# Gated linear attention, GLU and expert layer on one core: scans over four head pairs in one instruction, three more tiles turned by TensorE, low weight parts on VectorE, another opening order

## The chip, the cores and the metric

One core of a Trainium2 chip runs the whole program. The metric is device time in microseconds (us) from launch to end. The program has five engines that work in parallel and wait for each other by semaphores: PE (TensorE, matrix products), DVE (VectorE), ACT (ScalarE), POOL (GpSimd) and SP (SyncE), which issues the transfers between the main memory and the on-chip memory. Each engine takes its instructions strictly in the order in which the program holds them.

## The reference

Three layers follow one another on 4 sequences of 768 tokens with 8 heads of 48 features (3072 tokens of 384 features in all):

```
state = alpha[t] * state + outer(k[t], v[t])      # per head, 48 x 48
y[t]  = q[t] @ state
x  = rms_norm(y) * g
z  = (silu(x @ w_gate) * (x @ w_val)) @ w_out     # 384 -> 1536 -> 384
e  = argmax(z @ r_gate);  out = p_e * sigmoid((z @ r_ogate)[e]) * (relu(z @ w1[e]) @ w2[e])   # 8 experts
```

## The kernel before, in words

**Tiles.** The 3072 tokens are 24 tiles of 128. Three tiles form a group of 384 columns, so there are eight groups. Attention is computed in chunks: for a tile, the running products of alpha along its 128 tokens (backward `Z`, forward `A`) turn the recurrence into matrix products. q is multiplied by the forward product, k by the backward one; then come the scores (L392), the masked scores (L402), the output (L423, L427), the state (L448) and the normalised output turned round (L469), which feeds the GLU.

**Turning.** alpha, q and k must stand with features on partitions and the 128 tokens along the free dimension, four pairs of heads side by side (4 x 128 columns). Tiles 0 to 4 (`NAT` = 5) are loaded as rows, turned by PE with four products against the identity for each of a, k, q (L248, into the PSUM tile `ps_n`), and read from there. Tiles 5 to 23 are loaded in twelve blocks (`load_tile`) and turned by DVE (L344).

**Scans.** `after_scan` (L273) and `upto_scan` (L287) are scans of DVE, one for each pair of heads: four of 127 and four of 128 elements for a tile, with a product and a reciprocal of 4 elements between them (L281, L282).

**Weights.** The GLU's weights come as 36 chunks of 64-bit words. For each, DVE puts a float together (L491, L494, L497), ACT rounds it to the high part (L516, L543), and the low part is float minus high part. For chunks 4 to 17 (`LP` = (4, 18)) the low part is made by PE (L503 adds the float, L504 subtracts the high part, both into `ps_l`) and copied by ACT (L505); for the other 22 chunks DVE subtracts (L507). Each GLU product is three products: high by high, low by high, high by low (L571, L605).

**Order.** The first three tiles are written out by hand in `START` (a, r, k, q: turn and scan; s, n, y, d, x: score, key turn, output, state, turn of x; c: a step of conversions; w: idle products `junk` on PE). After that a loop over the GLU's products interleaves attention stages (`due`), steps of preparing later tiles (`PRN` for a slot) and steps of converting weights (`CR` for a slot). `SEATS` gives PSUM banks in the opening. A scheduler then orders each engine's instructions; the kinds in `K0` to `K2` keep the order in which they were written.

From about 640 us on the expert layer runs (L996, L997, L1012); the change doesn't touch it.

Of the kernel before, what the change touches and what calls it, by code (L numbers as in the profile page):

```python
# [8 lines left out]
F32 = mybir.dt.float32  # L9
# [3 lines left out]
AF = mybir.ActivationFunctionType  # L13
ALU = mybir.AluOpType
# [37 lines left out]
def gla_glu_moe_kernel(  # L52
# [29 lines left out]
    GT = 3  # L82
# [20 lines left out]
    ident = const.tile([P, P], F32, name="ident")  # L103
# [73 lines left out]
    for nm, pad in (("a", 1.0), ("q", 0.0), ("k", 0.0)):
        t_ = att.tile([P, NP, TW * D], F32, name=f"blk_{nm}")
        for r in (32, 96):
            nc.vector.memset(t_[r:r + 32, :, TW * D - 32:TW * D - 16], pad)  # L180
        blk[nm] = t_
# [18 lines left out]
    junk = [psM.tile([P, P], F32, tag='o2', name='junk')]  # L200
# [64 lines left out]
    SIDE = {(2, "A"): ("wgle", 0), (2, "qT"): ("wgle", 1), (2, "kT"): ("wgle", 2),  # L265
            (1, "aT"): ("wvhe", 0), (1, "P0"): ("wvhe", 1), (1, "P1"): ("wvhe", 2),
            (1, "kn"): ("wghe", 0), (1, "xn"): ("wghe", 1), (2, "v"): ("wghe", 2)}

    def after_scan(Z, al, p):

        pace('sc' + str(now[0]), nc.vector.tensor_tensor_scan(out=Z[:, p, P - 2::-1], data0=al[:, p, P - 1:0:-1],  # L273
                                                data1=ones_f.to_broadcast([P, P - 1]),
                                                initial=1.0, op0=ALU.mult, op1=ALU.mult))

    def ends(t, Z, al):

        en = att.tile([P, NP, 1], F32, tag="en", name="en", bufs=4)
        rc = att.tile([P, NP, 1], F32, tag="rc", name="rc", bufs=2)  # L280
        pace('sc' + str(now[0]), nc.vector.tensor_tensor(out=en, in0=al[:, :, 0:1], in1=Z[:, :, 0:1], op=ALU.mult))  # L281
        pace('sc' + str(now[0]), nc.vector.reciprocal(out=rc, in_=en))  # L282
        return en, rc

    def upto_scan(A, al, rc, p):

        pace('sc' + str(now[0]), nc.vector.tensor_tensor_scan(out=A[:, p, :], data0=al[:, p, :], data1=ones_f.to_broadcast([P, P]),  # L287
                                                initial=rc[:, p, :], op0=ALU.mult, op1=ALU.mult))

    QM, SM, LP = (CFG[x] for x in ("QM", "SM", "LP"))  # L290

    def prework_nat(t):
        Z = seat_of(t, "aT", [P, NP, P], CFG["ZBUF"])
        A = seat_of(t, "A", [P, NP, P], CFG["ABUF"])
        qT = seat_of(t, "qT", [P, NP, P], 2)
        kT = seat_of(t, "kT", [P, NP, P], 2)
        nc.gpsimd.memset(Z[:, :, P - 1:P], 1.0)
        ps = {}

        def turn_a():  # L300
            now[0] = t
            ps[0] = turn_nat(t, 0)
            for p in range(NP):
                after_scan(Z, ps[0], p)
            en, ps["rc"] = ends(t, Z, ps[0])
            pre[t] = (en, qT, kT)
# [25 lines left out]
    def prework(t):  # L332
        if t < NAT:
            w = prework_nat(t)
            for x in CFG['NO']:
                yield w[x]
            return
        aT = att.tile([P, NP, P], F32, tag="aT", name="aT", bufs=CFG["ZBUF"])
        Z = att.tile([P, NP, P], F32, tag="A", name="Z", bufs=CFG["ABUF"])
        qT = att.tile([P, NP, P], F32, tag="qT", name="qT", bufs=2)  # L340
        kT = att.tile([P, NP, P], F32, tag="kT", name="kT", bufs=2)

        def tr(dst, nm):
# [12 lines left out]
        for p in range(0, NP, 2):
            def sc(p=p):
                for pp in (p, p + 1):
                    after_scan(Z, aT, pp)
            yield sc  # L360

        def en():
            e_, ps["rc"] = ends(t, Z, aT)
            pre[t] = (e_, qT, kT)
        ps = {}
        yield en
        for p in range(0, NP, 2):
            def up(p=p):
                for pp in (p, p + 1):
                    upto_scan(aT, aT, ps["rc"], pp)  # L370
            yield up
# [948 lines left out]
```

## Time and profile before

| | us |
|---|---|
| median of 3 runs (lowest, highest) | 890.61 (889.08, 892.56) |
| the profiled execution's own time | 891.49 |
| its span, first to last instruction | 889.8 |
| PE busy in the span | 866.0 |
| DVE busy | 502.3 |
| ACT busy | 329.0 |
| POOL busy | 139.9 |

The span leaves out 1.69 us of the profiled execution's time around the first and last instruction. An instruction's duration overlaps with the next one's: what an instruction takes from its engine is read from one start to the next. [...]

### The profile page before, as it was taken

How to read it: one execution, taken by the hardware profiler on the slowest of the kernel's cores; microseconds unless marked ns; L12 is line 12 of the kernel's file. 1: busy time of each engine (PE TensorE's matmuls, PEld its weight loads, DVE VectorE, ACT ScalarE, POOL GpSimd, SP SyncE). 2: the span in 40 equal slices, each digit the busy share in tenths (PEclk: the TensorE clock that was granted, in tenths of full speed). 3: DMA queues.
4: the chain of work that ended last, by engine and by line, in shares of the span. 5: the costliest groups of instructions: out<-in, count | busy, mean ns of one | idle time of the engine just before them, and what ended most of it. 6: DMA issues, size and time to landing. Idle time of an engine off the chain costs nothing.

```text
span 889.8 us, 15748 instructions
## 1 busy us (share of the span) xinstructions
PE 866.0 (97%) x6048; PEld 826.0 (93%) x6048; DVE 502.3 (56%) x1181; ACT 329.0 (37%) x714; POOL 139.9 (16%) x175
## 2 busy tenths in 40 slices
PE   7999999999999999999999999999999999999994
PEld 6788899999999999999999999999998999999994
DVE  7679798558775655665675673244444443444330
ACT  1545554233333422332333343324234442445331
POOL 2000000000110010010010001013023343344331
PEclk7789999999999999999999999999999999999998
DMA  9825661637232222232222100005045264256510
GB/s 192 210 75 156 175 197 39 165 96 199 74 97 58 52 77 58 60 85 54 55 69 58 43 12 25 2 23 165 1 169 185 78 209 135 70 190 196 167 50 24
DMA packets 117485, 89.95 MB, mean 101 GB/s; under 512 B 49435, under 2 KB 112540, under 8 KB 117408
## 3 DMA queue, kind: packets, MB, share of 16 engines
q1 hardware_dynamic: 112944, 79.44, 33.5%
q0 software_dynamic: 4464, 9.48, 3.0%
q8 instruction: 48, 0.79, 0.4%
q14 instruction: 29, 0.24, 0.1%
HBM read 73.09 MB, written 16.07 MB: 100 GB/s over the span
## 4 chain that ended last, share of the span: by engine, by line
PE 86%; issue 4%; DMA 3%; DVE 2%; POOL 1%; ACT 1%; SPq 1%; POOLq 0%; ACTq 0%; DVEq 0%
PE ps_o L605 18%; PE ps_g L571 18%; PE ps_v L571 17%; PE ps_b L1012 8%; PE ps_h L571 7%; PE ps_s L392 4%; PE ps_y L427 3%; DMA st<-in_moe_w_dram 3%; PE ps_y L423 2%; PE ps_st L448 1%; PE ps_k L412 1%; PE ps_l L503 1%; PE ps_x L469 1%; SPq L880 1%; PE ps_n L248 1%
## 5 line engine op out<-in xcount | busy, mean ns | idle before, releaser
L582 DVE TENSOR_TENSOR tt<-tt,ps_v 128x384 f32<-128x384 f32 x96 | 52.8, 550 | 129.5 <-PE ps_v L571 122.6
L585 ACT ACTIVATE hh<-tt 128x384 fp32r<-128x384 f32 x96 | 50.2, 523 | 127.8 <-DVE tt L582 127.4
L563 ACT ACTIVATE tt<-ps_g 128x384 f32<-128x384 f32 x96 | 47.2, 492 | 127.5 <-PE ps_g L571 119.6
L571 PE MATMUL ps_g<-xh,wgh 128*128 128x384 f32 x192 | 68.5, 357 | 1.5 <-ACT xh L476 1.5
L1012 PE MATMUL ps_b<-w2a,h 128*128 128x384 f32 (+2 forms) x336 | 67.4, 339 | 1.3 <-ACT h L996 1.0
L997 DVE SCALAR_TENSOR_TENSOR h<-ps_h,h 128x256 fp32r<-128x256 f32 (+6 forms) x72 | 38.1, 531 | 52.7 <-ACT h L996 49.6
L571 PE MATMUL ps_v<-xh,wvh 128*128 128x384 f32 x192 | 67.3, 351 | 0.2 <-ACT wvh L516 0.2
L605 PE MATMUL ps_o<-wol,hh 128*128 128x400 f32 x192 | 66.7, 348 | 0.0
L605 PE MATMUL ps_o<-woh,hh 128*128 128x400 f32 x192 | 66.5, 355 | 0.0
L591 DVE TENSOR_TENSOR hl<-tt,hh 128x384 fp32r<-128x384 f32 x96 | 54.5, 567 | 21.0 <-ACT hh L585 20.4
L571 PE MATMUL ps_g<-xl,wgh 128*128 128x384 f32 x192 | 65.8, 343 | 0.0
L571 PE MATMUL ps_g<-xh,wgl 128*128 128x384 f32 x192 | 65.7, 342 | 0.0
L1012 PE MATMUL ps_b<-w2b,h 128*114 128x384 f32 (+3 forms) x336 | 65.2, 338 | 0.3 <-ACT h L996 0.2
L571 PE MATMUL ps_v<-xh,wvl 128*128 128x384 f32 x192 | 65.2, 340 | 0.0
L434 POOL TENSOR_SCALAR ss<-ss 128x1 f32<-128x1 f32 x24 | 5.0, 208 | 382.7 <-ACT xn L433 374.7
L571 PE MATMUL ps_v<-xl,wvh 128*128 128x384 f32 x192 | 64.8, 337 | 0.0
L605 PE MATMUL ps_o<-woh,hl 128*128 128x400 f32 x192 | 64.0, 344 | 0.0
L1012 PEld LDWEIGHTS ps_b<-w2a,h 128*128 128x128 f32 (+2 forms) x336 | 57.5, 181 | 2.5 <-ACT h L996 1.5
L1012 PEld LDWEIGHTS ps_b<-w2b,h 128*114 128x114 f32 (+3 forms) x336 | 57.4, 175 | 2.5 <-ACT h L996 1.0
L571 PE MATMUL ps_h<-x,w1b 128*128 128x456 f32 (+3 forms) x288 | 58.4, 343 | 0.6 <-DVE h L997 0.6
L996 ACT ACTIVATE h<-ps_h 128x256 fp32r<-128x256 f32 (+6 forms) x72 | 33.4, 468 | 63.5 <-PE ps_h L571 57.5
L571 PE MATMUL ps_h<-x,w1a 128*128 128x256 f32 (+3 forms) x288 | 53.4, 327 | 0.0
(279 smaller groups left out, 2029.7 us busy)
## 6 DMA issues: line engine op xcount, KB each, us to landing
st<-in_moe_w_dram SPq DMA_DIRECT2D x64, 384.0 KB
bucket<-zero SPq DMA_DIRECT2D x8, 772.0 KB
stg<-in_moe_w_gate_dram SPq DMA_DIRECT2D x12, 384.0 KB
stg<-in_moe_w_val_dram SPq DMA_DIRECT2D x12, 384.0 KB
stg<-in_moe_w_out_dram SPq DMA_DIRECT2D x12, 384.0 KB
v<-in_v_dram SPq DMA_DIRECT2D x23, 192.0 KB
blk_a<-in_alpha_dram SPq DMA_DIRECT2D x38, 96.0 KB
blk_q<-in_q_dram SPq DMA_DIRECT2D x38, 96.0 KB
```

The source lines that it names most:

```text
L392: nc.tensor.matmul(ps[hh][:, p, :], lhsT=kT[r, p, :], rhs=qT[r, p, :], start=True, stop=True)
L423: nc.tensor.matmul(ps[:, p * 2 * D:p * 2 * D + 2 * D], lhsT=qT[:, p, :], rhs=S_[:, p, :], start=(p == 0), stop=False, skip_group_check=True)
L427: nc.tensor.matmul(ps[u, h * D:h * D + D], lhsT=Pt[h % 2][:, h // 2, u], rhs=vt[t][:, h, :], start=first, stop=True, skip_group_check=True)
L563: nc.scalar.activation(tt, ps, AF.Silu)
L571: nc.tensor.matmul(ps, lhsT=a_[:, kc, :], rhs=b_[:, kc, :], start=(n == 0), stop=(n == 3 * KD - 1))
L582: nc.vector.tensor_tensor(out=tt, in0=tt, in1=ps, op=ALU.mult)
L585: nc.scalar.activation(hh, tt, AF.Copy)
L591: nc.vector.tensor_tensor(out=hl, in0=tt, in1=f(hh), op=ALU.subtract)
L605: nc.tensor.matmul(obank[s][i], lhsT=a_[:, sl], rhs=weight(b_, j), start=(j == j0 and n == 0), stop=(j == j1 - 1 and n == 2))
L996: nc.scalar.activation(hh[:, 0, :], ps, AF.Relu)
L997: nc.vector.scalar_tensor_tensor(out=hh[:, 1, :], in0=ps, scalar=0.0, in1=f(hh[:, 0, :]), op0=ALU.max, op1=ALU.subtract)
L1012: ins = nc.tensor.matmul(ob2[u][i][0:r], lhsT=hh[:, a_, sl], rhs=we[p][b_][:, j, :], start=(j == 0 and m == 0), stop=(j == KF2 - 1 and m = ...
```

## The change

The scans of the four head pairs become one: position 0 of each pair gets factor 0 in alpha's tile, and a second operand `begin`, zero elsewhere, sets the start value there (1 going backward, 1/Z going forward). Two small writes and a copy are added for it, and the forward scan of tiles 0 to 4 is written straight into q's tile, so that their tile `A` is gone. Tiles 5, 6 and 7 (`PET` = 8) are loaded as rows and turned by PE, copied out by ACT. `LP` is empty: all 36 low parts are made by DVE. The idle products have 512 columns instead of 128. `START`, `LOADS`, `SEATS`, `CR`, `PRN`, `TS`, `AHEAD` and the kept kinds are other numbers; one buffer instead of two for the backward products.

```diff
-    'START': 'a0 c r0 w6 a1 q0 k0 k1 r1 q1 w0 s0 s0 a2 c y0 s1 r2 k2 q2 y0 w0 s1 x0 y1 w4 y1 x1 ...',
+    'START': 'a0 r0 c a1 w6 q0 k0 k1 r1 q1 w0 s0 s0 a2 y0 s1 r2 c q2 y0 w0 s1 x0 k2 y1 w4 y1 x1 ...',
-    'LP': (4, 18),
+    'LP': (0, 0),
-    'AHEAD': 1,
+    'AHEAD': 0,
-    'CR': [3, 3, 3, 2],
-    'PRN': [1, 2, 1, 1],
+    'CR': [3, 4, 3, 4],
+    'PRN': [1, 2, 1, 2],
-    'ABUF': 2,
+    'ABUF': 1,
-    'TS': 2,
+    'TS': 3,
+    'PET': 8,
...
+    begin = att.tile([P, NP, P], F32, name="begin")
+    nc.gpsimd.memset(begin, 0.0)
...
-    def after_scan(Z, al, p):
-        ... nc.vector.tensor_tensor_scan(out=Z[:, p, P - 2::-1], data0=al[:, p, P - 1:0:-1],
-                                         data1=ones_f.to_broadcast([P, P - 1]), initial=1.0, op0=mult, op1=mult)
+    def after_scan(Z, al):
+        pace(k_, nc.vector.tensor_copy(en, al[:, :, 0:1]))
+        pace(k_, nc.vector.memset(al[:, :, 0:1], 0.0))
+        pace(k_, nc.vector.memset(begin[:, 1:, 0:1], 1.0))
+        pace(k_, nc.vector.tensor_tensor_scan(out=flat(Z)[:, W - 2::-1], data0=flat(al)[:, W - 1:0:-1],
+                                              data1=flat(begin)[:, W - 1:0:-1], initial=1.0, op0=mult, op1=add))
+        pace(k_, nc.vector.tensor_tensor(out=en, in0=en, in1=Z[:, :, 0:1], op=ALU.mult))
+    def upto_scan(A, Z, al):
+        pace(k_, nc.vector.reciprocal(out=begin[:, :, 0:1], in_=Z[:, :, 0:1]))
+        pace(k_, nc.vector.tensor_tensor_scan(out=flat(A), data0=flat(al), data1=flat(begin), initial=0.0,
+                                              op0=ALU.mult, op1=ALU.add))
...
         def tr(dst, nm):
+            if t < PET:
+                ps = bank([P, NP, P], "ps_n")
+                src = rowt[nm].rearrange("p (a h) d -> p a (h d)", h=2)
+                for p in range(NP):
+                    nc.tensor.transpose(ps[:, p, :], src[:, p, :], ident)
+                ins = nc.scalar.activation(dst, ps, AF.Copy)
+                if t + 1 < PET:
+                    load_tile(t + 1, nm)
+                return ins
...
+            nc.gpsimd.memset(Z[:, NP - 1, P - 1:P], 1.0)       # in prework, for every tile from 5 on
-            tc.keep_in_program_order(nc.tensor.matmul(junk[0], lhsT=ones_b, rhs=ones_b, start=True, stop=True))
+            ... nc.tensor.matmul(junk[0], lhsT=ones_b, rhs=ones_b.unsqueeze(1).to_broadcast([P, 4, P]), ...)
```

On PE, in the first rounds of GLU products after the opening (tile 3's output is `ps_y`, the next tile's turn `ps_n`), before:

```order
L423 MATMUL ps_y<-wide_134,qT 128x96 x4
L427 MATMUL ps_y<-v,P_647 64x48 x8
L427 MATMUL ps_y<-v,P_649 64x48 x8
L248 MATMUL ps_n<-ident,nat 128x128 x4
L503 MATMUL ps_l<-F,ident 128x384
L504 MATMUL ps_l<-wvh,minus 128x384
L571 MATMUL ps_v<-xh,wvl 128x384
L605 MATMUL ps_o<-woh,hh 128x400
```

and now, from the same output on:

```order
L447 MATMUL ps_y<-wide_125,qT 128x96 x4
L451 MATMUL ps_y<-v,P_593 64x48 x8
L451 MATMUL ps_y<-v,P_595 64x48 x8
L270 MATMUL ps_n<-ident,nat 128x128 x4
L595 MATMUL ps_v<-xh,wvh 128x384
L595 MATMUL ps_v<-xl,wvh 128x384
```

The pair that makes a low part is gone from here and from thirteen more places. Some rounds later on PE stand the first of the nine new turns, between products of a GLU round (`row_a` is alpha's tile 5 as rows):

```order
L595 MATMUL ps_g<-xh,wgh 128x384
L595 MATMUL ps_g<-xl,wgh 128x384
L416 MATMUL ps_s<-qT,kT 128x128 x4
L371 MATMUL ps_n<-ident,row_a 128x128 x4
L595 MATMUL ps_g<-xh,wgl 128x384
L595 MATMUL ps_g<-xh,wgh 128x384
```

Before, no instruction of PE stood there; DVE turned that tile. On DVE, the first instructions after the constants, before (`aT` holds the backward product of tile 0, `side` that of tile 1, `A` the forward ones):

```order
L273 SCALAR_TENSOR_TENSOR aT<-ps_n,ones_f 128x127 x4
L281 TENSOR_TENSOR en<-ps_n,aT 128x4
L282 RECIPROCAL rc<-en 128x4
L287 SCALAR_TENSOR_TENSOR A<-ps_n,rc,ones_f 128x128 x4
L273 SCALAR_TENSOR_TENSOR side<-ps_n,ones_f 128x127 x4
L320 TENSOR_TENSOR qT<-qT,A 128x512
L317 TENSOR_TENSOR kT<-ps_n,aT 128x512
```

and now:

```order
L302 COPY en<-ps_n 128x4
L303 MEMSET ps_n 128x4
L304 MEMSET begin 128x3
L305 SCALAR_TENSOR_TENSOR aT<-ps_n,begin 128x511
L308 TENSOR_TENSOR en<-en,aT 128x4
L314 RECIPROCAL begin<-aT 128x4
L315 SCALAR_TENSOR_TENSOR qT<-ps_n,begin 128x512
```

Eight scans have become two, and three small instructions stand ahead of the first of them. On POOL, in the stretch of tiles 6 and 7 (`ss` is a tile's mean square, which ACT's scaling waits for), before:

```order
L1107 IOTA tab 128x22
L1124 IOTA tab 128x1
L1126 IOTA tab 128x3
L1128 IOTA tab 128x8
L434 TENSOR_SCALAR ss<-ss 128x1
L435 TENSOR_TENSOR ss<-ss,mhalf 128x1
```

and now:

```order
L392 MEMSET Z 128x1
L1132 IOTA tab 128x22
L1149 IOTA tab 128x1
L1151 IOTA tab 128x3
L1153 IOTA tab 128x8
L184 MEMSET blk_a 32x4x16 x2
L184 MEMSET blk_k 32x4x16 x2
L184 MEMSET blk_q 32x4x16 x2
L392 MEMSET Z 128x1
L458 TENSOR_SCALAR ss<-ss 128x1
L459 TENSOR_TENSOR ss<-ss,mhalf 128x1
```

A one-element write into the next tile's `Z`, which must wait until DVE has used the `Z` before it, has come ahead of a tile's `ss`, and the writes of padding into the block tiles of tile 8 as well.

## Rows read from the trace of the kernel before

**Rows 1.** The page's parts 1 and 2: busy time, and the granted clock by slices.
```profile
PE 866.0 (97%) x6048; PEld 826.0 (93%) x6048; DVE 502.3 (56%) x1181; ACT 329.0 (37%) x714; POOL 139.9 (16%) x175
...
PEclk7789999999999999999999999999999999999998
```

**Rows 2.** Windows view: stretch, its length, busy us (instructions) by engine, clock, DMA.
```profile
20.00:30.00 10.00, 10.00 (x78) 8.29 (x77) 9.38 (x21) 4.53 (x12) 0.82 (x3) 0.50 1.10 178
30.00:40.00 10.00, 8.60 (x95) 7.51 (x93) 4.02 (x8) 5.17 (x15) 1.89 (x4) 0.72 0.87 255
40.00:50.00 10.00, 7.98 (x62) 6.63 (x61) 9.52 (x25) 6.05 (x15) 0.11 (x1) 0.79 0.55 146
70.00:80.00 10.00, 9.64 (x52) 8.17 (x51) 9.74 (x23) 4.09 (x11) 0.00 (x0) 0.83 0.64 162
...
120.00:140.00 20.00, 20.00 (x124) 19.88 (x123) 18.70 (x43) 9.30 (x22) 0.00 (x0) 1.00 0.49 154
...
200.00:250.00 50.00, 50.00 (x405) 47.90 (x405) 39.82 (x107) 16.74 (x39) 5.28 (x8) 1.00 0.50 128
```

**Rows 3.** Timeline of PE before the GLU stream: start, us, instruction, [idle before <-releaser].
```profile
38.78 0.67 PE L448 MATMUL ps_st<-side,kn 128*64 128x48 f32 x16 [1.40 <-ACT kn L414]
...
45.17 0.44 PE L571 MATMUL ps_g<-xh,wgh 128*128 128x384 f32 x1 [1.48 <-ACT xh L476]
...
46.32 2.08 PE L392 MATMUL ps_s<-qT,kT 48*128 48x128 f32 x16 [0.54 <-DVE qT L317]
...
49.10 0.67 PE L571 MATMUL ps_g<-xl,wgh 128*128 128x384 f32 x1
```

**Rows 4.** Timeline of PE: the first and the last pair for a low part.
```profile
39.88 0.81 PE L503 MATMUL ps_l<-F,ident 128*128 128x384 f32 x2
40.23 0.64 PE L504 MATMUL ps_l<-wvh,minus 128*128 128x384 f32 x1
40.71 0.74 PE L536 MATMUL pc<-wr,wT 128*128 128x16 f32 x6
...
111.19 0.94 PE L503 MATMUL ps_l<-Fo,ident 128*128 128x400 f32 x2
111.97 0.49 PE L528 MATMUL pt<-ident,Fo 128*128 128x128 f32 x3
112.22 0.43 PE L504 MATMUL ps_l<-woh,minus 128*128 128x400 f32 x1
112.49 0.71 PE L605 MATMUL ps_o<-woh,hh 128*128 128x400 f32 x3
```

**Rows 5.** Timeline of PE: four turns in a row, and what starts next.
```profile
81.35 0.60 PE L412 MATMUL ps_k<-ident,kT 128*128 128x128 f32 x4
81.79 0.49 PE L528 MATMUL pt<-ident,Fo 128*128 128x128 f32 x3
```

**Rows 6.** Timeline of PE: the four idle products inside the opening.
```profile
29.73 0.61 PE L781 MATMUL junk<-ones_b 128*128 128x128 bf16 x4
30.27 2.07 PE L392 MATMUL ps_s<-side 48*128 48x128 f32 x8
```

**Rows 7.** Timeline of DVE, tile 0's scans and the start of tile 1's.
```profile
5.20 1.36 DVE L273 TENSOR_TENSOR_SCAN aT<-ps_n,ones_f 128x127 f32<-128x127 f32 x4 [2.70 <-PE ps_n L248]
...
7.00 1.61 DVE L287 TENSOR_TENSOR_SCAN A<-ps_n,rc,ones_f 128x128 f32<-128x128 f32 x4
8.52 1.33 DVE L273 TENSOR_TENSOR_SCAN side<-ps_n,ones_f 128x127 f32<-128x127 f32 x4
```

**Rows 8.** Groups of instructions on DVE: busy us, mean ns | idle before.
```profile
L344 DVE STREAM_TRANSPOSE aT<-blk_a 128x512 f32<-128x512 f32 x19 | 20.8, 1097 | 0.1
L507 DVE TENSOR_TENSOR wgl<-F,wgh 128x384 fp32r<-128x384 f32 x4 | 2.2, 553 | 0.0
```

**Rows 9.** Timeline of ACT: tile 7's scaling.
```profile
194.37 0.58 ACT L436 ACTIVATE xn<-ps_y,ss 128x384 f32<-128x384 f32 x1 [0.51 <-POOL ss L435]
```

**Rows 10.** Timeline of PE: the turn that reads it.
```profile
198.12 0.49 PE L469 MATMUL ps_x<-ident,xn 128*128 128x128 f32 x3
```

More of the change, by code (lines that the diff above doesn't have):

```diff
@@ L20 @@
 CFG = {
-    'START': 'a0 c r0 w6 a1 q0 k0 k1 r1 q1 w0 s0 s0 a2 c y0 s1 r2 k2 q2 y0 w0 s1 x0 y1 w4 y1 x1 s2 s2 y2 y2 x2 n0 n2 c x2 n1 l l d0 c d2 w0 x0 d1 d1 x1 d2 d0',
-    'LOADS': 'a0 q0 a1 k0 q1 k1 a2 v0 w g k2 v1 q2 w w r w w v2 w w w w',
-    'SEATS': (3, 5, 4, 6, 3, 2, 0, 5, 0, 2, 4, 4, 2, 3, 3, 2, 6, 1, 4, 5, 4, 2, 2, 2, 6, 3, 0, 2, 6, 4),
+    'START': 'a0 r0 c a1 w6 q0 k0 k1 r1 q1 w0 s0 s0 a2 y0 s1 r2 c q2 y0 w0 s1 x0 k2 y1 w4 y1 x1 s2 s2 y2 y2 x2 n1 n0 c n2 l l x2 d1 d0 c d2 w0 x0 x1 d2 d1 d0',
+    'LOADS': 'a0 q0 a1 k0 q1 k1 a2 v0 w g k2 v1 q2 w w w r w v2 w w w w',
+    'SEATS': (3, 5, 4, 6, 1, 1, 0, 5, 0, 2, 4, 4, 5, 3, 3, 2, 6, 1, 4, 4, 4, 2, 2, 1, 6, 3, 0, 6, 6, 4),
     'QM': 'vddddd',
     'SM': 'dad',
[4 rows of a table removed]
-    'AHEAD': 1,
[4 rows of a table added]
+    'AHEAD': 0,
     'PREP6': 9,
-    'CR': [3, 3, 3, 2],
-    'PRN': [1, 2, 1, 1],
+    'CR': [3, 4, 3, 4],
+    'PRN': [1, 2, 1, 2],
     'JS': 6,
-    'ABUF': 2,
+    'ABUF': 1,
     'ZBUF': 1,
@@ L176, in gla_glu_moe_kernel, with blocks @@
     blk = {}
[L177 to L181, printed above, removed]
+    PADS = {"a": 1.0, "q": 0.0, "k": 0.0}
+    def blocks():
+        for nm, pad in PADS.items():
+            t_ = att.tile([P, NP, TW * D], F32, tag=f"blk_{nm}", name=f"blk_{nm}")
+            for r in (32, 96):
+                nc.gpsimd.memset(t_[r:r + 32, :, TW * D - 32:TW * D - 16], pad)
+            blk[nm] = t_
     BS = B - 1
@@ L199, in gla_glu_moe_kernel @@
     spread = [True]
-    junk = [psM.tile([P, P], F32, tag='o2', name='junk')]
+    junk = [psM.tile([P, 4, P], F32, tag='o2', name='junk')]
     paced = [CFG['K0']]
@@ L217, in bank, with load_tile @@
         return psA.tile(shape, F32, tag="att", name=name)
-    LEAD = 2 * GT
-    def load_tile(t):
+    rowt = {}
+    def load_tile(t, nms="aqk"):
         b, c = place_of[t]
         t0 = c * P
+        if t < PET:
+            for nm in nms:
+                if nm not in rowt:
+                    t_ = att.tile([P, 2 * NP, 64], F32, tag=f"blk_{nm}", name=f"row_{nm}")
+                    nc.gpsimd.memset(t_[:, :, D:], PADS[nm])
+                    rowt[nm] = t_
+                src = {"a": alpha, "q": q, "k": k}[nm]
+                nc.sync.dma_start(rowt[nm][:, :, 0:D], src[b, :, t0:t0 + P, :].rearrange("h p d -> p h d"))
+            return
+        if not blk:
+            blocks()
         for nm, src in (("a", alpha), ("q", q), ("k", k)):
+            if nm not in nms:
+                continue
             dst = blk[nm]
@@ L232, in gla_glu_moe_kernel @@
     NAT = CFG['NAT']
+    PET = CFG['PET']
     nat = [wpool.tile([P, 3, 2 * NP, 64], F32, tag=nm, name="nat") for nm in ("wohe", "wole", "wvle")]
@@ L263, in seat_of @@
         return att.tile(shape, F32, tag=nm, name=nm, bufs=bufs)
-    SIDE = {(2, "A"): ("wgle", 0), (2, "qT"): ("wgle", 1), (2, "kT"): ("wgle", 2),
+    SIDE = {(2, "aT"): ("wgle", 0), (2, "qT"): ("wgle", 1), (2, "kT"): ("wgle", 2),
             (1, "aT"): ("wvhe", 0), (1, "P0"): ("wvhe", 1), (1, "P1"): ("wvhe", 2),
             (1, "kn"): ("wghe", 0), (1, "xn"): ("wghe", 1), (2, "v"): ("wghe", 2)}
-    def after_scan(Z, al, p):
-        pace('sc' + str(now[0]), nc.vector.tensor_tensor_scan(out=Z[:, p, P - 2::-1], data0=al[:, p, P - 1:0:-1],
-                                                data1=ones_f.to_broadcast([P, P - 1]),
-                                                initial=1.0, op0=ALU.mult, op1=ALU.mult))
@@ L277, in ends @@
-    def ends(t, Z, al):
-        en = att.tile([P, NP, 1], F32, tag="en", name="en", bufs=4)
[L280 to L288, printed above, removed]
@@ L290, in gla_glu_moe_kernel, with flat @@
-    QM, SM, LP = (CFG[x] for x in ("QM", "SM", "LP"))
+    def flat(x):
+        return x.rearrange("p a b -> p (a b)")
+    def after_scan(Z, al):
+        en = att.tile([P, NP, 1], F32, tag="en", name="en", bufs=4)
+        W = NP * P
+        k_ = 'sc' + str(now[0])
+        pace(k_, nc.vector.tensor_copy(en, al[:, :, 0:1]))
+        pace(k_, nc.vector.memset(al[:, :, 0:1], 0.0))
+        pace(k_, nc.vector.memset(begin[:, 1:, 0:1], 1.0))
+        pace(k_, nc.vector.tensor_tensor_scan(out=flat(Z)[:, W - 2::-1], data0=flat(al)[:, W - 1:0:-1],
+                                              data1=flat(begin)[:, W - 1:0:-1], initial=1.0,
+                                              op0=ALU.mult, op1=ALU.add))
+        pace(k_, nc.vector.tensor_tensor(out=en, in0=en, in1=Z[:, :, 0:1], op=ALU.mult))
+        return en
@@ L292, in prework_nat @@
+    def upto_scan(A, Z, al):
+        k_ = 'sc' + str(now[0])
+        pace(k_, nc.vector.reciprocal(out=begin[:, :, 0:1], in_=Z[:, :, 0:1]))
+        pace(k_, nc.vector.tensor_tensor_scan(out=flat(A), data0=flat(al), data1=flat(begin), initial=0.0,
+                                              op0=ALU.mult, op1=ALU.add))
+    LP = CFG['LP']
     def prework_nat(t):
         Z = seat_of(t, "aT", [P, NP, P], CFG["ZBUF"])
-        A = seat_of(t, "A", [P, NP, P], CFG["ABUF"])
         qT = seat_of(t, "qT", [P, NP, P], 2)
@@ L296, in prework_nat @@
         kT = seat_of(t, "kT", [P, NP, P], 2)
-        nc.gpsimd.memset(Z[:, :, P - 1:P], 1.0)
+        nc.gpsimd.memset(Z[:, NP - 1, P - 1:P], 1.0)
         ps = {}
@@ L302, in turn_a @@
             ps[0] = turn_nat(t, 0)
[L303 to L306, printed above, removed]
+            pre[t] = (after_scan(Z, ps[0]), qT, kT)
         def up():
             now[0] = t
-            for p in range(NP):
-                upto_scan(A, ps[0], ps["rc"], p)
+            upto_scan(qT, Z, ps[0])
         def turn(x, dst, by, mode):
@@ L323, in turn @@
             return go
-        return {"a": turn_a, "r": up, "k": turn(1, kT, Z, "d"), "q": turn(2, qT, A, QM[t])}
+        return {"a": turn_a, "r": up, "k": turn(1, kT, Z, "d"), "q": turn(2, qT, qT, "d")}
     def load_v(t):
@@ L343, in tr @@
         def tr(dst, nm):
+            if t < PET:
+                ps = bank([P, NP, P], "ps_n")
[6 more added lines that the diff above has]
+                return ins
             return nc.vector.transpose(out=dst.rearrange("a p (c j) -> a p j c", j=TW),
@@ L348, in tr_qk @@
             tr(qT, "q")
-            if t + 1 < NTILE:
+            if PET <= t + 1 < NTILE:
                 load_tile(t + 1)
@@ L352, in tra, with sc @@
             now[0] = t
-            pace(f'sc{t}', tr(aT, 'a'))
+            ins = tr(aT, 'a')
+            if t >= PET:
+                pace(f'sc{t}', ins)
         yield tra
         yield tr_qk
[L356 to L371, printed above, removed]
+        def sc():
+            now[0] = t
+            nc.gpsimd.memset(Z[:, NP - 1, P - 1:P], 1.0)
+            pre[t] = (after_scan(Z, aT), qT, kT)
+        yield sc
+        yield lambda: upto_scan(aT, Z, aT)
         def mul(o, i):
             pace('km%d' % t, nc.vector.tensor_tensor(out=o, in0=o, in1=i, op=ALU.mult))
-        yield lambda: mul(kT[:, :, 0:P - 1], Z[:, :, 0:P - 1])
+        yield lambda: mul(kT, Z)
         yield lambda: mul(qT, aT)
@@ L780, in warm @@
         for _ in range(n):
-            tc.keep_in_program_order(nc.tensor.matmul(junk[0], lhsT=ones_b, rhs=ones_b, start=True, stop=True))
+            tc.keep_in_program_order(nc.tensor.matmul(junk[0], lhsT=ones_b, rhs=ones_b.unsqueeze(1).to_broadcast([P, 4, P]),
+                                                      start=True, stop=True))
     begun, after, steps = {}, {}, {}
```

6 rows, old and new, of the table CFG are left out of this document.

## The prediction

> **What bounds the kernel now.** I read the page's busy times first: PE is at work 866.0 of the 889.8 us, and from the fourth of 40 slices on (67 us) its granted clock stays at nine tenths or more [rows 1]. Then the windows view, for where PE is not the bound. From 200 to 250 us PE is busy 50.00 of 50.00 at clock 1.00 [rows 2]: there time is saved only by taking instructions from PE. The expert layer runs the same instructions in both kernels, so the change has to win or lose in the first 150 us. [...] The timeline of PE names the gaps: it waits 1.40 us for ACT's copy of a turned key, 1.48 for the first high part of x, 0.54 for DVE's q, and the GLU's stream begins at 49.10 us [rows 3]. So each part is priced by two questions: what leaves PE's stream after 49 us, and when that stream begins.
>
> **Low parts on DVE (LP).** Fourteen chunks lose two PE instructions and an ACT copy each. Start to start, the first pair takes 0.83 us (39.88 to 40.71); the last takes 1.05, 0.78 and 0.27 with a turn between them [rows 4]. From the first to the last, the fourteen pairs sum to 13.0 us, 0.93 in the mean. Thirteen of them lie behind 49.10 us in a stream that waits next to never, so I take all 13.0 us; the least is 12.2, without the first pair, which lies among the waits. In exchange DVE gets 14 subtractions of 553 ns [rows 8], 7.7 us, each behind ACT's rounding. They cost nothing as long as DVE stays ahead of PE. What speaks for that: from 120 to 140 us the old kernel already makes its low parts on DVE, DVE is busy 18.70 of 20, and PE still 20.00 of 20.00 [rows 2].
>
> **Tiles 5 to 7 turned by PE (PET).** PE gets 9 times four turns. [...] DVE loses nine turns of 1097 ns [rows 8], 9.9 us, which more than pays for the 7.7 above in the same stretch (50 to 150 us). ACT gets nine copies of 512 columns and loses fourteen of 384; it is busy 37% [rows 1] and I put this at nothing. SP issues three transfers of a tile instead of twelve, so the weights queued behind them go out earlier.
>
> **Scans in one instruction.** For tile 0, four backward scans begin at 5.20 and the forward four end their turn at 8.52: 3.32 us, of which the backward four with the two small instructions are 1.80 and the forward four 1.52 [rows 7]. The merged scans run over 511 and 512 elements, which no row shows. A scan over as many elements in one instruction instead of four takes at most 1.36 to 1.61 us, as the four do [rows 7]; at the rate of a subtraction of 384 (553 ns [rows 8]) 512 would be 0.74. I take 1.15 each, nearer the rows of the scans themselves. With five small instructions (0.7 us in all, from the 0.44 that the old two leave between the scans) a tile costs 3.0 instead of 3.3: DVE gains 0.3 us for a tile, 7 us in all, between a loss of 0.6 and a gain of 1.1 for a tile. From 80 us on PE hides it. In the opening the first key product comes later in DVE's order, behind tile 1's backward scan too, so the first score starts no earlier; I count 0 there.
>
> [...]
>
> **Wider idle products.** Ten products have four times the columns. The first six fall while DVE still scans tile 0, to 8.52 [rows 7], and the first score waits for that: they cost nothing. The four in the opening take 0.54 us now, 29.73 to 30.27 [rows 6]; four times that is 2.2, so 1.6 more. [...]
>
> **Order of the opening.** Counted in the two orders, PE has the same turns, scores, outputs and state products ahead of the GLU's stream, less one low-part pair and with wider idle products. So only the waits can move: 3.42 us of them before 49.10 [rows 3]. The rounding that stood ahead of x's high part on ACT comes behind it now, DVE has one tile's scans less ahead of the first GLU result, and two weight chunks are converted later. I take 1.5 us back, between 3.4 won and 4 lost. The clock I leave as it is: nothing in an order says when it rises.
>
> **The sum.** 13.0 off, 4.0 on, 1.2 on, 1.5 off: 9.3 us. The profiled execution took 891.49 us, so 882.2; it lies 0.88 above the median of the runs shown, 890.61, so a median of 881.3.
>
> **Rivals.** First, the clock comes up early. [...] Chance 0.12.
>
> Second, the gain goes back in the opening. The low clock lasts until after the stream has begun: its first 8 us take twice as long, 4 us, and the waits grow by the 4 of my bound in place of 1.5 less: 881.3 + 8 = 889, no difference. For it: from 40 to 50 us, around the waits for x and q, the clock has a mean of 0.79 [rows 2, 3], so it fell again there, and the same chain is still in place. Against it: PE's work ahead of the stream is no more than before. Chance 0.2.
>
> Third, slower: DVE becomes the bound between 50 and 130 us. Its low parts wait for ACT in DVE's fixed order, and behind each stand the next product of gate and value, its low part and the masked scores, for which PE waits. From 40 to 50 and 70 to 80 us DVE is already at 9.52 and 9.74 of 10 [rows 2]. It decides when DVE's work there exceeds PE's shortened stretch, which wants merged scans of 1.8 us instead of 1.15, or eight rounds with 1 us of waiting; each gap can drop the clock too, as at 70 to 80, for 1.7 us. Eight such rounds and four drops are 15 us: 881.3 + 15 = 896. Against it stands 120 to 140 us. Chance 0.1.
>
> Fourth, POOL: the one-element writes into `Z` stand ahead of a tile's `ss` and wait for DVE. Tile 7's scaling ended at 194.95 and its turn on PE started at 198.12 [rows 9, 10]: 3.2 us to spare, so such a wait must be longer than that to be seen. Fourteen tiles with 1 us beyond it would give 895. Chance 0.03.
>
> **The numbers.** My forecast (877 to 886) has 0.55, with the four rivals 0.12, 0.2, 0.1 and 0.03. A difference of 0.5%, about 4.5 us, is what a measurement of this kernel can tell from none: faster is below 886.1, slower above 895.1. Faster is the forecast and the first rival, 0.67; the second rival and a part of the slower ones that ends short of their price make 0.2; slower is 0.13. The range of 8 in 10 goes from 871, where the early clock meets the bounds of the terms, to 892, past the second rival. The forecast's own range is 877 to 886.
>
> **What would show it.** `ps_l` gone and PE's busy time down by some 8 us; the nine new turns at 0.4 to 0.5 us for four; a merged scan between 1.05 and 1.3 us; PE still without waits from 80 to 640 us; the GLU's stream starting between 46 and 50 us; DVE's busy time in 50 to 150 us no higher than before. The prediction is wrong if PE waits for DVE's low parts or for `ss`, if the stream starts later than 53 us, or if the clock falls more often behind 50 us than the one time it does now.

## The result, and the profile after

The changed kernel takes 877.84 us in the median of 4 runs (875.78 to 880.26), the kernel before 890.23 in the same comparison; the ratio is 0.9859, with a 95% interval of 0.9823 to 0.9895. It is 12.4 us faster, within the range that was given and 3.5 us below the predicted time. The profiled execution took 880.26 us, 11.2 less than the profiled one before; it is the slowest of the four, two of which took 879.25 and 880.26 us at a mean granted clock of 0.989 and 0.990, and two 875.78 and 876.42 at 0.996 and 0.995.

The page after shows the same engine as the bound, 10 us less of it, and a clock that is at nine tenths or more in every slice but the first and the last; these lines answer to [rows 1]. `PEclk` is PE's granted clock as a share of the full one: the traces of before and after record the levels 1.00 and 0.50 alone, and values between are means over a stretch (the digits are tenths).

```profile
PE 856.1 (97%) x6042; PEld 814.5 (93%) x6042; DVE 489.3 (56%) x1108; ACT 326.0 (37%) x708; POOL 143.8 (16%) x204
...
PEclk8999999999999999999999999999999999999998
```

The windows view of after, for the stretches of [rows 2]: stretch, length, busy us (instructions) of PE, PEld, DVE, ACT and POOL, granted clock, DMA share, GB/s.

```profile
20.00:30.00 10.00, 8.82 (x76) 6.47 (x73) 8.16 (x18) 5.39 (x15) 0.75 (x2) 0.75 1.03 167
30.00:40.00 10.00, 9.23 (x130) 7.56 (x130) 8.28 (x19) 5.86 (x18) 0.83 (x3) 1.00 0.87 220
40.00:50.00 10.00, 10.00 (x91) 9.78 (x91) 10.00 (x25) 6.99 (x14) 1.24 (x2) 1.00 0.50 152
70.00:80.00 10.00, 10.00 (x77) 9.08 (x76) 9.54 (x22) 6.05 (x16) 1.18 (x2) 1.00 0.61 176
120.00:140.00 20.00, 20.00 (x133) 19.70 (x133) 14.01 (x30) 9.23 (x21) 1.02 (x7) 1.00 0.15 31
200.00:250.00 50.00, 50.00 (x402) 47.46 (x401) 34.31 (x88) 17.47 (x42) 7.86 (x13) 1.00 0.29 78
```

From 40 us on PE is at work at full clock, with one wait of 0.6 us up to the end of the GLU's stream at 628 and DVE at 10.00 of 10 beside it at first. Before, PE had gaps until 50 us and low clocks until 80. The timeline of PE after, at the place of [rows 3]: start, us, instruction, [idle before <-releaser].

```profile
35.42 0.63 PE L270 MATMUL ps_n<-ident,nat 128*128 128x128 f32 x4 [0.70 <-PE ps_n L270]
...
37.04 1.16 PE L416 MATMUL ps_s<-qT,kT 48*128 48x128 f32 x16
...
38.77 0.44 PE L595 MATMUL ps_g<-xh,wgh 128*128 128x384 f32 x1
...
39.37 0.45 PE L595 MATMUL ps_g<-xl,wgh 128*128 128x384 f32 x1
```

The first GLU product stands at 38.77 instead of 45.17, and its second input at 39.37 instead of 49.10; the three waits of [rows 3] are gone. On DVE, the merged scans of tile 0 take the place of [rows 7] (timeline), and the groups of scans and low parts stand beside [rows 8] (busy us, mean ns | idle before).

```profile
5.72 1.22 DVE L305 TENSOR_TENSOR_SCAN aT<-ps_n,begin 128x511 f32<-128x511 f32 x1
...
7.27 1.22 DVE L315 TENSOR_TENSOR_SCAN qT<-ps_n,begin 128x512 f32<-128x512 f32 x1
8.41 0.14 DVE L302 COPY en<-ps_n 128x4 f32<-128x4 f32 x1
```
```profile
L305 DVE TENSOR_TENSOR_SCAN Z<-aT,begin 128x511 f32<-128x511 f32 x19 | 23.2, 1222 | 0.6
L315 DVE TENSOR_TENSOR_SCAN aT<-aT,begin 128x512 f32<-128x512 f32 x19 | 23.1, 1217 | 0.1
...
L531 DVE TENSOR_TENSOR wvl<-F,wvh 128x384 fp32r<-128x384 f32 x8 | 4.4, 552 | 0.0
```

Where the time went is read by adding up PE's steps: each product from its start to the start of the next, by what it writes, so that a wait counts with the product ahead of it. "Chunk 11" is the first value product with the eleventh of the twelve chunks of `w_val`.

| stretch of PE's stream | before | after | difference | the largest terms |
|---|---|---|---|---|
| to the first GLU product | 45.2 | 38.8 | -6.4 | scores -3.5, turns -1.8, `ps_k` -1.3, `ps_l` -0.8, idle products +2.0 |
| from there to chunk 11 | 91.8 | 74.9 | -16.8 | `ps_l` -12.2, GLU -2.9, scores -1.7 |
| chunk 11 to the last `ps_o` | 502.8 | 514.2 | **+11.4** | scores **+5.5**, GLU **+2.9**, new turns +2.3 |
| the rest | 238.1 | 238.7 | +0.6 | |

So 23 us are won by chunk 11, and half of that is lost again in a stretch where PE never waits. The predicted terms account for some 12 of the 23 and, with six of the nine new turns, for 2.3 of the 11.4 given back.

One caution for all that follows: the view counts PEclk as 1.00 until the first level that the trace records, at 7.9 us here. Before that the clock is told by PE's steps: a turn's product takes 0.21 us to the next at 0.50 and 0.11 at 1.00, and up to there they take 0.21.

### The profile page after: what moved, and what is told of

Its sections match the earlier page's. It is cut to its first block, busy times and chain, and to the rows that moved or that the text cites. A ratio compares the mean times of both kernels' runs of the same rounds, so it can differ in the third digit from the quotient of the medians.

```text
span 878.6 us, 15655 instructions
## 1 busy us (share of the span) xinstructions
PE 856.1 (97%) x6042; PEld 814.5 (93%) x6042; DVE 489.3 (56%) x1108; ACT 326.0 (37%) x708; POOL 143.8 (16%) x204
## 4 chain that ended last, share of the span: by engine, by line
PE 85%; DMA 5%; issue 4%; DVE 2%; POOL 1%; ACT 1%; SPq 1%; POOLq 0%; DVEq 0%; ACTq 0%
PE ps_o L629 18%; PE ps_v L595 18%; PE ps_g L595 18%; PE ps_b L1037 8%; PE ps_h L595 7%; PE ps_s L416 4%; PE ps_y L451 3%; DMA st<-in_moe_w_dram 3%; PE ps_y L447 2%; DMA er<-bucket 1%; PE ps_st L472 1%; PE ps_k L436 1%; PE ps_x L493 1%; POOL out_dram L1053 1%; PE pc L560 1%
```

## Experiments

All ratios are to the kernel before, measured beside each run.

**E1. The scores held together.** From 140 to 540 us, the windows view of the score products alone (`ps_s`): PE's busy time and the count of records, first of before, then of after.

```profile
140.00:540.00 400.00, 21.04 (x272) 17.02 (x272) 21.81 (x34) 1.00 0.29 75
```
```profile
140.00:540.00 400.00, 26.49 (x258) 19.61 (x258) 20.67 (x32) 1.00 0.30 77
```

Fewer records take more time. A tile's timeline tells why: in after the products are parted, and GLU products stand between.

```profile
316.44 0.34 PE L595 MATMUL ps_g<-xh,wgl 128*128 128x384 f32 x1
316.71 0.48 PE L416 MATMUL ps_s<-qT,kT 48*128 48x128 f32 x2
317.12 0.44 PE L595 MATMUL ps_v<-xh,wvh 128*128 128x384 f32 x1
...
320.29 0.34 PE L629 MATMUL ps_o<-woh,hl 128*128 128x400 f32 x1
320.56 1.16 PE L416 MATMUL ps_s<-qT,kT 48*128 48x128 f32 x14
321.64 0.45 PE L595 MATMUL ps_g<-xh,wgh 128*128 128x384 f32 x1
```

Each product leaves two records. The operands of the two heads of a pair stand on partitions 0 to 47 and 64 to 111 (`slice(64 * hh, 64 * hh + D)`), and a record has 48 active rows. Side by side, a record of the one starts 6 or 7 ns after one of the other, and the next two 105 ns later: 0.22 us for two products, 1.09 for the tile. The lone product here takes 0.41 us, and the one left without a partner at the end of the fourteen records 0.31: 1.50 us for the tile. The fourteen records take 1.09 us here, as long as all sixteen do when they stand together. So the whole loss of 0.41 is the product that stands apart, and 0.2 more lies in the GLU products next to it (0.27 and 0.28 in place of 0.17 each).

```
 for p in range(NP):
     for hh in range(2):
-        nc.tensor.matmul(ps[hh][:, p, :], ...)
+        ins = nc.tensor.matmul(ps[hh][:, p, :], ...)
+        if t >= GT:
+            tc.keep_in_program_order(ins)
```

> The kernel after, with the eight score products of a tile held in the order they are written from the fourth tile on, so that from the sixth tile on all eight stand side by side on TensorE as they do before the change. Theory (the scheduler's order parts them, and a score product that stands alone loses its partner in the other half of the array's rows): the steps of the score products after the tenth weight chunk go back from 1.45 to about 1.1 us a tile (-5.5 us over 18 tiles), and the GLU's runs that they cut get up to 3 us back; 869.5 to 872.5 us against 877.8 of after. Rival (the lead melts after the tenth chunk because something else holds TensorE there, the steps are only where it shows): within 2 us of 877.8, and the steps of another tile grow by what the scores give back.

Measured: 867.71 us (866.66 to 870.77, 5 runs), ratio 0.9742 (0.9722 to 0.9761), 10 us below after. The same view of this kernel:

```profile
140.00:540.00 400.00, 19.75 (x272) 16.50 (x272) 21.87 (x34) 1.00 0.31 76
```

Behind chunk 11 the scores give back 6.5 us, the GLU runs that they cut 2.4 and `ps_x` 0.9: 9.8, more than expected, and no other tile grows. The theory holds in that standing apart is what costs; no run parts whole pairs, so how much of it is the missing partner is not shown. What makes the scheduler part them was not settled: they are parted in the same way in the orders that come of E2, E3 and E4, whose opening, lists or low parts differ.

**E2. Narrow idle products.**

```
-matmul(junk[0], lhsT=ones_b, rhs=ones_b.unsqueeze(1).to_broadcast([P, 4, P]), ...)
+matmul(junk[0][:, 0, :], lhsT=ones_b, rhs=ones_b, ...)
```

> The kernel after, with the idle products of the opening 128 columns wide as before the change. The scheduler also puts the first two tiles' scores as twice four, as before. Theory (the wide idle products at 23.3 to 25.0 us are what lifts the granted clock at 25): the clock stays at its low level until about 35 us, the GLU stream starts 3 to 8 us later than 39.4, time 881 to 886 us. Rival (the order of the opening gives the gain, the idle products have no part in it): clock back at full by 26 us, stream start within 1.5 us of 39.4, time 876.5 to 879.

Measured: 889.36 us (12 runs), 0.9972 (0.9953 to 0.9991). The loss is larger than either expected. The clock goes much as the theory has it: its first recorded level is 1.00 from 28.05 us on, and until then PE runs at 0.50, as its steps show. Eight products of a turn take 1.94 us at 10 us (PE's timeline), where after takes 1.06 (shown under E7).

```profile
10.24 1.94 PE L270 MATMUL ps_n<-ident,nat 128*128 128x128 f32 x8 [1.01 <-DMA nat<-in_k_dram]
```

The GLU's second product, the theory's mark of the stream, starts at 44.88, 5.5 us later than in after, as expected. About half of that is another thing: the order that the scheduler made puts the `xl` that this product needs late on DVE, and PE stands, after which the clock falls again (the windows, then PE's timeline):

```profile
40.00:45.00 5.00, 1.85 (x24) 1.24 (x23) 5.00 (x12) 2.84 (x9) 0.10 (x1) 1.00 0.80 215
45.00:50.00 5.00, 5.00 (x26) 4.75 (x28) 3.52 (x8) 2.30 (x3) 0.00 (x0) 0.66 0.39 103
```
```profile
44.88 0.51 PE L595 MATMUL ps_g<-xl,wgh 128*128 128x384 f32 x1 [2.69 <-DVE xl L501]
```

To the first GLU product it loses 2.8 us against after, from there to chunk 11 another 7.3. How the loss divides between the idle products and the new order is not settled here; whether the width itself has a part is E10's question.

**E3. The opening's lists of before** (START, LOADS, SEATS, K0; the rest as after).

> The kernel after, with the list of the opening's steps, of its loads, of its banks and of the paced operations (START, LOADS, SEATS, K0) of before; scans, idle products, low parts and turns as after. Theory (the order of the opening gives the 9.7 us by which the GLU stream starts earlier): the stream starts at 46 to 49 us, time 884 to 887. Rival (the idle products' width and the merged scans give it): stream start at 39.5 to 43 us, time 878 to 881.

Measured: 891.31 us (12 runs), 1.0008 (0.9993 to 1.0022): the whole gain of the change is gone. The GLU's second product, by which theory and rival count, stands at 44.1 us, between the 39.5 to 43 of the one and the 46 to 49 of the other, so the theory had the place only half right. To the first product 3.9 us are lost, from there to chunk 11 another 8.2 (GLU steps +6.3, with waits for `xh` and `xl` and a lower clock), behind it none. Its windows have the clock low where after has 1.00:

```profile
25.00:30.00 5.00, 5.00 (x30) 3.19 (x30) 3.15 (x7) 3.17 (x10) 0.75 (x2) 0.50 1.35 179
30.00:35.00 5.00, 5.00 (x36) 4.36 (x37) 1.34 (x3) 1.69 (x5) 0.00 (x0) 0.50 1.13 269
...
45.00:50.00 5.00, 5.00 (x26) 4.91 (x25) 4.99 (x12) 1.86 (x5) 0.10 (x1) 0.77 0.66 205
```

**E4. Low parts on PE again** (LP (4, 18)).

> The kernel after, with the low parts of 14 weight chunks made by TensorE again (LP 4 to 18). Theory (prediction's term: a pair of ps_l products holds TensorE for 0.93 us and nothing hides it): +13 us, 889 to 892. Rival (part of these pairs lies in idle time of TensorE, or DVE gets relief from it): +8 us or less, under 886.

Measured: 889.16 us (12 runs), 0.9986 (0.9968 to 1.0003), +11.3 against after. In PE's steps the pairs are 11.9 us between the stream's start and chunk 11. The term of the sum holds, a little below its 13.0.

**E5. Scans apart again**, on E1 (eight scans a tile with reciprocals as before).

> As e1_scores_kept (867.7 us), but with a scan for each pair of heads again, eight a tile, with their ends and reciprocals as before; all else as there. Theory (prediction's: the merged scans pay only where DVE is what the opening waits for): DVE gets about 2.2 us more a tile, the first three tiles stand in the opening, so the GLU stream starts 2 to 6 us later than 38.8 and from the tenth weight chunk on nothing changes; 870 to 874 us. Rival (DVE has idle time enough in the opening too): within 1 us of 867.7. Second rival (DVE, full in 40 to 80 us, holds TensorE up there as well): over 875.

Measured: 875.80 us (872.61 to 876.23, 5 runs), 0.9827 (0.9815 to 0.984), +8.1 against E1. The time is that of the second rival. The stream starts no later (38.4), and the profiled run, the fastest of the five, loses 4.5 us from there to chunk 11, where PE waits 1.30 us for `xl` and 0.66 for ScalarE's `tt`. DVE's busy time is only 8.0 us higher over the run (495.8 against 487.8), not 2.2 a tile. The two profiles are only 1.8 us apart, since E1's is the slowest of its five. PE's order differs too, from the first scores on. How much of the 8 is the scans and how much the new order stays open.

**E6. Tiles 5 to 7 turned by DVE again**, on E1 (PET 5).

> As e1_scores_kept (867.7 us), but tiles 5 to 7 are turned by DVE again (PET 5). Theory (a turn of four products costs TensorE 0.37 to 0.44 us, nine of them, and DVE's transposes hide): -3.3 to -4.0 us, 863.7 to 864.4. Rival (DVE, busy 9.5 to 10 of every 10 us until 80 us, turns them late, so that scores wait): 867 or more, with TensorE waits on DVE between 50 and 130 us.

Measured: 879.55 us (4 runs), 0.9861 (0.9843 to 0.9879): **+11.8** against E1, although PE is rid of nine turns. The rival holds, though from 50 to 130 us PE waits for a weight and an `xl` and not for scores. Its windows, and two waits in PE's timeline:

```profile
50.00:60.00 10.00, 10.00 (x75) 9.11 (x76) 10.00 (x23) 4.26 (x12) 0.00 (x0) 1.00 0.77 186
60.00:70.00 10.00, 8.09 (x72) 6.84 (x72) 10.00 (x21) 3.43 (x8) 0.10 (x1) 0.75 0.41 112
70.00:80.00 10.00, 10.00 (x65) 9.34 (x64) 7.04 (x16) 4.53 (x12) 0.74 (x2) 0.57 0.77 186
```
```profile
63.49 0.44 PE L597 MATMUL ps_v<-xh,wvh 128*128 128x384 f32 x1 [1.69 <-ACT wvh L542]
...
100.59 0.69 PE L597 MATMUL ps_g<-xl,wgh 128*128 128x384 f32 x1 [1.96 <-DVE xl L503]
```

DVE is full for 20 us, PE waits for a weight whose conversion stands on DVE behind a tile's scan and key product (58.61 to 62.34), and behind the gap the clock is at the lower level for part of the time up to 80 us. E1's DVE is as full from 40 to 80 us (39.7 of 40) and PE does not wait there, so fullness alone is not it: in E6 six turns of 1.1 us stand in DVE's order by 70 us as well. From the stream's start to chunk 11 the loss is 15.0 us; behind it PE has its 2.6 us back.

**E7. Idle products fill a gap**, on E1 (`w8 q0 k0` in place of `w6 q0 k0`).

> As e1_scores_kept (867.7 us), but with eight wide idle products in place of six ahead of the first tile's q turn, so that TensorE does not stand for 0.63 us before the k turn at 10.2 us. In e1_scores_kept the clock is at its low level from 14.7 to 25 us, in e4_low_parts_back with the same order of the opening at its full level throughout, and its TensorE had no such gap. Theory (that gap goes with the fall): clock at full level from 10 to 25 us, the GLU stream starts near 35.6 and not 38.8, -2.5 to -3.2 us: 864.5 to 865.2. Rival (the gap has nothing to do with it): clock low from about 15 to 25 us all the same, 867 to 868.5.

Measured: 866.97 us (866.73 to 869.32, 5 runs), 0.9734 (0.9719 to 0.9749). In the profile the clock is full and the stream starts at 35.56, as the theory has it; by the medians it is 0.7 us faster than E1, and the intervals overlap. The gain in time is not shown. By chunk 11 the profile has 1.5 of the 3.3 us left, as PE then waits 2.30 us for `xl`. The five executions of E1 say why the medians agree: only the profiled one, 870.77 us, has a mean clock of 0.988; the other four have 0.994 to 0.996 and took 866.7 to 868.2. So the fall does not come in every execution of E1 (whether PE stood in those four is not known), and one profile of each kernel can't show that the two more products prevented it. PE's timeline ahead of the scores and the windows behind them, first of after, then of E4, then of E7:

```profile
10.22 1.06 PE L270 MATMUL ps_n<-ident,nat 128*128 128x128 f32 x8 [0.63 <-DMA nat<-in_k_dram]
```
```profile
15.00:20.00 5.00, 5.00 (x52) 4.46 (x53) 4.03 (x11) 1.57 (x4) 0.76 (x2) 0.50 1.19 286
20.00:25.00 5.00, 5.00 (x42) 3.48 (x38) 3.87 (x9) 1.89 (x7) 0.75 (x2) 0.50 0.95 170
```
```profile
9.63 1.62 PE L270 MATMUL ps_n<-ident,nat 128*128 128x128 f32 x12
```
```profile
15.00:20.00 5.00, 4.97 (x83) 4.04 (x83) 4.96 (x12) 2.32 (x7) 0.77 (x2) 1.00 1.18 285
20.00:25.00 5.00, 3.56 (x33) 2.62 (x32) 5.00 (x13) 3.41 (x10) 0.75 (x2) 1.00 0.86 136
```
```profile
10.50 1.47 PE L270 MATMUL ps_n<-ident,nat 128*128 128x128 f32 x12
```
```profile
15.00:20.00 5.00, 4.35 (x69) 3.67 (x67) 5.00 (x13) 1.57 (x4) 0.76 (x2) 1.00 1.18 282
20.00:25.00 5.00, 3.11 (x37) 2.12 (x36) 5.00 (x12) 3.75 (x12) 1.05 (x2) 1.00 0.94 161
```

**E8. The low parts alone, in the kernel before** (LP (0, 0)).

> The kernel before with one edit: the low parts of all weight chunks on DVE (LP 0 to 0). Theory (the pairs of ps_l products hold TensorE for 13.0 us and nothing else changes): 877 to 879.5 us. Rival (14 more subtractions of 0.55 us on DVE between 40 and 130 us come late for the weights): over 881, with TensorE waits on DVE's low parts there.

Measured: 886.65 us (6 runs), 0.9953 (0.9939 to 0.9967): 4.4 us, a third of the price on PE. The rival holds. All 13.0 us of `ps_l` are gone from PE, and its GLU steps grow by 5.1 up to chunk 11, where it waits for what DVE makes (windows, then a wait in PE's timeline):

```profile
70.00:80.00 10.00, 8.72 (x64) 8.10 (x63) 10.00 (x24) 4.70 (x12) 0.00 (x0) 1.00 0.55 135
80.00:90.00 10.00, 8.80 (x100) 7.61 (x99) 10.00 (x24) 5.52 (x16) 0.74 (x2) 1.00 0.66 160
```
```profile
77.72 0.45 PE L605 MATMUL ps_o<-wol,hh 128*128 128x400 f32 x1 [1.28 <-DVE wol L507]
```

**E9. The third tile's low part sooner**, on E7 (in START, `n1 n0 n2 l l x2 d1 d0 c c d2` in place of `n1 n0 c n2 l l x2 d1 d0 c d2`).

> As e7_idle_fill (867.0 us), with one conversion step of the opening's list moved: in e7 the third tile's xl waits behind conversions of a w_out chunk on DVE, which themselves wait for that chunk's DMA, and the GLU stream stands 2.3 us for it at 36.2 us; now xl is written ahead of those conversions but one. Theory (that queue on DVE is the wait): the stream's wait falls to 1 us or less, 865.5 to 866.3. Rival (what the stream gets earlier it gives back waiting for the first weights): within 0.7 us of 867.0.

Measured: 870.93 us (5 runs), 0.9783 (0.9753 to 0.9812), 4 us slower. The wait for `xl` is gone, as expected, and PE stands 2.35 us for `xh` ahead of the first product instead, then 0.65 for a tile's q; the clock is at 0.66 from 35 to 40. Neither theory had that.

**E10. Narrow idle products, as many columns**, on E7 (four of 128 for each of 512; all else in the same order).

> As e7_idle_fill (867.0 us), with four idle products 128 columns wide in place of each one 512 wide; every other instruction stands in the same order on TensorE, DVE and ScalarE. Theory (the width of the idle products is nothing by itself, what e2_narrow_idle lost it lost by another order): 866.0 to 868.0 us, GLU stream from 35.6 to 36.2 us, clock full from 10 to 25 us. Rival (the wide products hold the clock up): clock low in 15 to 25 us, stream start 3 us later, 869 to 870.

Measured: 869.00 us (867.96 to 871.09, 5 runs), 0.9748 (0.973 to 0.9766). The clock is full from 10.4 to 37 us and the stream starts at 35.5, so the width by itself is not what brings the clock up or holds it, and E2's 11.5 us came with its order or its fewer columns. The time falls in the rival's range, but its intervals and E7's overlap, so the 2 us are not shown. In the profile the clock is low from 37.7 to 41.1, after a wait of 2.04 for `xl`; E7 waits 2.30 there and keeps its clock. Why stays open. That costs 1.0 us by chunk 11; of the 2.9 between the two profiles 1.9 lie in the expert layer, which the edit doesn't touch.

**E11. Turns and low parts both undone**, on E1 (PET 5, LP (4, 18)).

> As e1_scores_kept (867.7 us), with both of these edits undone: tiles 5 to 7 are turned by DVE and the low parts of 14 weight chunks are made by TensorE. Apart, they cost +11.8 (e6_fewer_turns against e1_scores_kept) and +11.3 us (e4_low_parts_back against after). Theory (DVE's time between 40 and 130 us is what they share: with the low parts off DVE, its transposes hide again): 867.7 + 11.3 - 3.4 = 875.6, 874 to 878 us. Rival (the turns cost what they cost whatever DVE has): 867.7 + 11.3 + 11.8 = 890.8, 888 us or more.

Measured: 879.38 us (4 runs), 0.9865 (0.9846 to 0.9883). Added up, the two edits undone would be 890.8; the pair costs 11.7, what the low parts cost alone. With the low parts off DVE, putting the turns back costs next to nothing, so the 11.8 of E6 is DVE's time, and the order on it, and not the turns'. The same three runs show the low parts from the other side: with the turns on DVE, moving the low parts there gains nothing either (E6 879.55, E11 879.38), although PE loses 12.7 us of `ps_l`. The 3.4 us that the theory let PE win are not there: PE still waits once for a masked score of DVE (1.61 us at 65.56).

## Why the prediction was right in the sum and wrong in its parts

**Low parts, -13.0.** On PE, 13.0 measured by its steps, and 11.3 by E4, with the turns on PE. But the sentence that they "cost nothing as long as DVE stays ahead of PE" was carried by 120 to 140 us, a stretch in which DVE turned no tiles. In the kernel before it fails (E8), and in E6: the third rival, at a chance of 0.1, has the mechanism of this edit without the turns.

**Turns, +4.0.** The 4.0 of the sum is nine times the 0.44 us that four products of a turn took at a granted clock of 1.00 (81.35 to 81.79, [rows 5]). Two turns in a row take 0.47 and 0.36 us after (117.32 to 118.15); all nine sum to 3.4 by their steps, near the term. What the term left out is what they buy: with the low parts on DVE they keep 15 us of waits and low clock away (E6, E11). The prediction said that they "more than pay" for DVE's new work and gave that no price. So the two parts had to be priced as one.

**Scans.** 1.22 us for 1.15, and 3.08 us for a tile (5.33 to 8.41) against 3.0. The 1.22 us for 511 or 512 elements is under the 1.36 to 1.61 of the four scans and over the 0.74 that a subtraction's rate gave: 2.4 ns for an element, where the subtraction of 384 in 552 ns takes 1.4. That DVE's gain is hidden is put in doubt by E5, which loses 4.5 us behind the stream's start, the new order's share not separated.

**Idle products, +1.2.** The four in the opening take 1.66 us (23.34 to 25.00) in place of 0.54 [rows 6], so 1.1 more; with the first six it is 2.0. No run shows the 1.2 of the sum. At the lower level a product takes four times as long to the next with 512 columns as with 128, 0.43 us (23.74 to 24.16) against 0.11 (six from 4.95 to 5.59 before), and the 0.54 holds 0.24 from the last one's start to the next score's (30.03 to 30.27). The theory of E2 lets them lift the clock: it did come up early, at 25 us. E10 takes the width out of it. With fewer columns (E2) it came up only at 28 us, though in another order, so whether the columns have a part is not shown.

**Order of the opening, -1.5.** This is the step that failed: a few sentences counted instructions and moved only three waits, and "the clock I leave as it is" put the clock at nothing. Measured beside `ps_l` are -5.6 to the first GLU product and -4.6 from there to chunk 11; these hold the idle products' +2.0 and three of the nine new turns, +1.1, so the order itself has -13.3. Part of it is the clock: behind 10 us PE is at the lower level for 34 us before and for 10 after (14.7 to 25.0). Tile 3's scores, paired alike in both, took 2.08 us [rows 3] and take 1.16 (37.04). An estimate from [rows 2] of what the low clock took of PE's busy time from 30 us on is 8.60 x 0.28 + 7.98 x 0.21 + 9.64 x 0.17 = 5.7 us (busy time by what the mean clock lacks), so the first rival came in part, on top of the forecast. Part is pairing: tile 2's scores stood in two runs of 2.0 us at 0.50 (25.65 and 30.27) and stand side by side in 1.09 at 1.00 (26.45), where two runs apart take 1.1 each (57.84 and 59.83). Undoing the lists (E3) gives back 12.0 us up to chunk 11, with 31 us at the lower level. No run changes the order and keeps the clock, so their shares stay open.

**"The same instructions" behind 80 us.** The other failure, which has no term: the prediction took every kept product to cost what it did, and never looked at which stood beside which. That is +9.1 us against before, and holding the scores together takes 9.8 away (E1). The errors are some 12 us one way and 9 the other; that 9.3 came near 11.2 is owed to that, and is luck.

The second rival (stream late) and the fourth (POOL) did not come: the stream is early, and PE has no wait for `ps_x` behind 40 us. Two of the prediction's own signs missed: the stream starts at 39.4 us, ahead of its 46 to 50, and DVE's busy time from 50 to 150 us is 89.4 in place of 86.0, not lower.

## What to carry to other kernels

Price a move of work between engines together with every other move that uses the same engine in the same stretch: with E1's lists the low parts alone gain nothing (E6 against E11) and the turns alone some 0.4 (an estimate: E1 plus E4's 11.3, against E11), while together they gain 11.7 (E11 against E1). Each of four parts undone by itself (E2, E3, E4, E6) takes back 11 to 14 us, about the whole gain, so such prices don't add up; the lists were not set anew for any of them, and what a part is worth with lists of its own is not shown. When a scheduler writes the order, compare for each engine what stands beside what, even in stretches where nothing was changed and nothing waits; adding up start-to-start steps by tile finds what busy times hide. Where a small product takes less time beside another than alone (here 0.22 us for two, and 0.31 to 0.41 for a lone one), hold them side by side by hand: that one edit gave 10 us, and E1 and E7, with it, are the fastest kernels here at 867 to 868 us. Check a clock that a view reports against the steps of like products.

## What the runs showed of the hardware

Score products with 48 rows, on partitions 0 to 47 and 64 to 111, start 6 to 7 ns apart when they stand side by side, and two cost 0.22 us where a lone one takes 0.31 to 0.41. The steps of the GLU products around the lone score at 316.71 are 0.27 us into it and 0.28 behind it, where they are 0.17 to 0.18 among themselves; no run isolates what takes the 0.1.

The clock's level in 15 to 25 us differs between profiles with the same order of PE in the opening (after 0.50, E4 1.00), and is worth 3.2 us at the stream's start (38.77 against 35.61). It differs between executions of one kernel too, by the times and mean clocks of after and E1. By PE's steps every profile starts at the lower level: the first turns last 2.03 to 2.08 us for seven products or 1.08 to 1.09 for four, where eight at the full level last 1.06 (after, at 10.22). The first rise comes at 7.7 to 10.6 us in the ten whose idle products have 512 columns, or as many in narrow ones (E10). In the three with fewer columns it comes at 8.3 us and lasts 3.4 (before), at 37.45 (E8, with the same opening but for a low part) and at 28.05 (E2).

Before the low stretches of before, after, E1 and E5, PE had stood 0.57 to 0.79 us ahead of the k turn at 10.1 to 10.3 us; in E4, E6, E7, E9, E10 and E11, full throughout up to 35 us, it had not. But E3, which did not stand there, fell at 16.6 us, and E7, E9 and E10 stood 0.5 to 1.1 us at 12.6 us and kept their clock; E2 and E8 tell nothing of it, as theirs had not yet risen. So that is no rule, and the cause stays open.
